# A planned order for attention ahead of a mixture of experts: two more names in the planner's port set, and attention's tables of numbers replaced

## The chip, the cores and the metric

The kernel runs on one core of a Trainium2 chip. The metric is the device time of one execution in microseconds (us). The engines are named as in the profile: PE (TensorE; PEld is its weight load), DVE (VectorE), ACT (ScalarE), POOL (GpSimd) and SP (SyncE, which here issues nearly all DMAs from one queue).

## The reference

Attention over 8 batches, 8 heads, 576 positions and 64 columns, joined with a memory, and then a layer of 8 experts with a capacity.

```
scores = scale * q @ k^T, causal;  a = exp(scores - max);  a /= a.sum + 1e-9
local = a @ v
phi(x) = where(x > 0, x, exp(x) - 1) + 1          # = max(x, 0) + exp(min(x, 0))
q_p = phi(q);  mem = (q_p @ M_prev) / (q_p . z_prev + 1e-6)
attn = g * mem + (1 - g) * local                  # g from beta, by head
x = attn as [4608, 512];  logits = x @ w_gate
experts take tokens in order of logits, 576 at most each;  out = relu(x @ w1) @ w2
```

## The kernel before, in words

Attention goes through 16 units, each half a batch (4 heads). All values are carried as two float16 parts, a high one and the low rest, so each product is made of two or three matmuls. For a unit, k, q and v are loaded (`kf`, `qf`, `vf`); k, q and phi(q) are cast to the high part, the low part is taken by a subtraction on POOL (`h<-kf,h`, `p<-ef,p`), both are turned by PE into `pb` (five PSUM banks shared by all stages) and copied to `kT`, `qT` and `pT`. The half of `qT` that holds q's high part is moved to the lower 64 partitions of `qM` (the step `qmove`), k's low part likewise to `kB` (the step `kb`). Row maxima come from PE products in `pb` and DVE reductions (`mx<-pb`, the steps MX); they are turned, cast to `mr` (the step `mfin2r`) and sent by a DMA into row 64 of `qM`. Then come the scores in `pb`, their exponentials on ACT (`ph<-pb`, `pb<-pb` or `pf<-pb`), the low parts on DVE (`pl<-pb,ph`) or POOL (`pl<-pf,ph`), the products with v (`avo`) and with the memory (`avm`), and the division and sum on DVE. The result is cast to `xs` (the step `ncast`) and written to DRAM.

Four small steps matter for what follows. `phr` writes relu(-q) into `ef`; `phe` (ACT) takes the exponential of its negative and `phs` (DVE) adds max(q, 0), which gives phi. `mh` casts the merged memory and z to float16 on 64 partitions; `mh2` copies that to the other 64; `ml` subtracts it for the low part.

The order is made by a planner in the kernel's own program. Each step is a node with its inputs, alternatives of engine with a planned duration each, and a priority. `Sched.run` places the nodes one after the other on planned clocks: among those that could start within `tol` ns of the earliest it takes the lowest priority. The order so found is the order of the instructions on every engine; at run time each engine only waits for its data. Priorities come from tables (`off` by step, `dl` by unit and step), the engine of a step with alternatives from `pin` (one letter for each use in a unit: a = ACT, v = DVE, p = POOL, d = a DMA of SP, * = the planner chooses, by durations and `bias`). Unit 0 has no pins.

The planner also holds DVE and POOL apart. For a step whose name is in the set `LK`, a start on DVE is not placed before POOL's last planned step has ended (`poolb`), and POOL's next is not placed before that step's end (`lockV`). Steps whose names are not in `LK` are planned on DVE as if POOL were not there.

The expert layer is a second plan with tables of its own, which follows attention's.

Of the kernel before, what the change touches and what calls it, by code (L numbers as in the profile page):

```python
# [24 lines left out]
          'kba': -38256.38,  # L25
          'kbd': -26666.66,
          'kbv': -40060.57,
          'kha': 14508.09,
          'khp': 79231.15,
          'khv': 24617.63,  # L30
          'klp': -1086.28,
          'klv': 16564.27,
          'mh2a': 20115.95,
          'mh2v': -71452.4,
          'mha': 22820.34,
          'mhv': 89368.52,
          'mlp': -31325.33,
          'mlv': 98087.6,
          'mra': 17856.1,
          'mrv': -40742.45,  # L40
          'mza': 48409.13,
          'mzv': 168176.88,
          'nap': -923.34,
          'nav': -3267.9,
          'nca': -18457.66,
          'ncp': 25373.91,
          'ncv': -21886.13,
          'nsp': -32165.33,
          'nsv': -132.24,
          'p2p': 3448.83,  # L50
          'p2v': -5.41,
          'p4sp': -101839.76,
          'p4sv': 7041.96,
          'pha': -31945.75,
          'php': 29271.45,
          'phra': -17422.93,
          'phrv': 21464.53,
          'phv': -15662.98,
          'plp': -19639.54,
          'plv': 43456.26,  # L60
          'prepca': -6518.9,
          'prepcv': -117462.96,
          'qha': -48927.36,
          'qhp': 53729.35,
          'qhv': -70868.4,
          'qlp': 66042.22,
          'qlv': 67290.35,
          'qmovea': 37764.26,
          'qmoved': 9935.43,
          'qmovev': -17228.33,  # L70
          'tea': -3203.28,
          'tev': -3567.68,
          'vha': -7856.47,
          'vhp': 10605.02,
          'vhv': 49945.15,
          'vlp': 20772.25,
          'vlv': 26630.93,
          'xtea': -71403.73,
          'xtev': 179859.67},
 'dl': {'0': {'AV': 146.09,  # L80
              'MX': -624.92,
              'N': -126.83,
              'P2': 205.25,
              'S': -143.66,
              'fin1': 261.98,
              'fin2': 110.94,
              'kb': -92.85,
              'kh': -1057.1,
              'kl': -799.26,
              'kt': 409.38,  # L90
              'lk': -815.63,
              'lm': -128.09,
              'lq': -615.68,
              'lv': 17.6,
              'maxrem': -253.86,
              'mfin': 482.24,
              'mfin2': 105.89,
              'mfin3': -298.67,
              'mh': -569.13,
              'ml': 141.3,  # L100
              'mz': -906.61,
              'nadd': -161.05,
              'ncast': 1096.75,
              'nsub': -761.84,
              'ph': -9.18,
              'phe': -815.32,
              'phr': 503.82,
              'phs': 98.73,
              'pl': -713.0,
              'prep': 158.29,  # L110
              'proc24': 786.98,
              'pt': 498.84,
              'qh': -300.16,
              'ql': -10.8,
              'qmove': 271.64,
              'qt': -259.45,
              'sj4': -1617.95,
              'vh': 583.59,
              'vl': 580.19},
        '1': {'AV': -25.95,  # L120
              'MX': -64.68,
              'N': -535.37,
              'P2': -147.0,
              'S': 748.22,
              'fin1': 664.4,
              'fin2': -3.45,
              'kb': 238.53,
              'kh': -839.21,
              'kl': 952.34,
              'kt': 230.67,  # L130
              'lk': -445.86,
              'lm': -581.61,
              'lq': -148.4,
              'lv': 20.94,
              'maxrem': 246.5,
              'mfin': -687.39,
              'mfin2': 22.77,
              'mfin3': -21.79,
              'mh': -646.37,
              'ml': 320.58,  # L140
              'mz': 193.71,
              'nadd': -884.82,
              'ncast': -314.9,
              'nsub': 431.22,
              'ph': 77.88,
              'phe': -364.63,
              'phr': -979.48,
              'phs': 202.3,
              'pl': 390.55,
              'prep': 112.67,  # L150
              'proc24': 17.02,
              'pt': 120.82,
              'qh': -827.23,
              'ql': 1226.18,
              'qmove': 922.01,
              'qt': -359.08,
              'sj4': -517.69,
              'vh': -449.25,
              'vl': -525.9},
        '10': {'AV': 733.61,  # L160
               'MX': -9.55,
               'N': -43.6,
               'P2': -27.07,
               'S': 120.09,
               'fin1': -121.61,
               'fin2': 528.74,
               'kb': 308.28,
               'kh': 579.55,
               'kl': 231.8,
               'kt': -310.65,  # L170
               'lk': -985.15,
               'lm': 22.19,
               'lq': -760.75,
               'lv': 653.54,
               'maxrem': 832.59,
               'mfin': -154.75,
               'mfin2': -103.77,
               'mfin3': 164.76,
               'mh': 1180.68,
               'ml': -110.56,  # L180
               'mz': 442.55,
               'nadd': -95.12,
               'ncast': 113.49,
               'nsub': -253.87,
               'ph': 370.77,
               'phe': 1372.58,
               'phr': -862.17,
               'phs': 266.25,
               'pl': -166.72,
               'prep': 671.38,  # L190
               'proc24': 43.6,
               'pt': -134.43,
               'qh': 380.29,
               'ql': 824.81,
               'qmove': 110.84,
               'qt': -905.38,
               'sj4': -117.53,
               'vh': 1303.13,
               'vl': 73.67},
        '11': {'AV': 392.77,  # L200
               'MX': -119.89,
               'N': 107.93,
               'P2': -1287.85,
               'S': 537.41,
               'fin1': 559.45,
               'fin2': 175.23,
               'kb': -23.13,
               'kh': -316.63,
               'kl': 316.7,
               'kt': -267.79,  # L210
               'lk': 1004.46,
               'lm': 317.64,
               'lq': 927.07,
               'lv': -555.69,
               'maxrem': -231.11,
               'mfin': 53.44,
               'mfin2': -28.5,
               'mfin3': -375.62,
               'mh': 289.75,
               'ml': -252.17,  # L220
               'mz': -107.18,
               'nadd': 309.19,
               'ncast': -1234.73,
               'nsub': 691.93,
               'ph': -604.12,
               'phe': -723.96,
               'phr': -499.8,
               'phs': -516.33,
               'pl': 169.21,
               'prep': -551.37,  # L230
               'proc24': 438.49,
               'pt': -289.42,
               'qh': 420.7,
               'ql': 540.55,
               'qmove': 441.27,
               'qt': -164.57,
               'sj4': 108.12,
               'vh': -419.32,
               'vl': -35.56},
        '12': {'AV': 92.79,  # L240
               'MX': 85.32,
               'N': 713.16,
               'P2': -217.09,
               'S': -90.99,
               'fin1': 335.64,
               'fin2': 663.47,
               'kb': 1548.9,
               'kh': 225.74,
               'kl': -192.86,
               'kt': -292.84,  # L250
               'lk': -226.47,
               'lm': -572.91,
               'lq': -787.24,
               'lv': 475.0,
               'maxrem': 222.28,
               'mfin': 289.39,
               'mfin2': 383.96,
               'mfin3': 442.07,
               'mh': 272.14,
               'ml': 221.9,  # L260
               'mz': 444.22,
               'nadd': -589.26,
               'ncast': 297.69,
               'nsub': 743.62,
               'ph': -132.61,
               'phe': 153.97,
               'phr': 393.16,
# [1546 lines left out]
```

## Time and profile before

| | |
|---|---|
| time, median of 3 runs | 937.16 us (933.75 to 937.4) |
| profiled execution, its own time | 931.03 us |
| its span | 929.3 us |
| DVE busy, whole span | 693.6 us (75%) |
| PE busy, whole span | 804.9 us (87%) |
| POOL busy, whole span | 589.6 us (63%) |
| ACT busy, whole span | 579.3 us (62%) |

Attention takes the first 450 us or so, the expert layer the rest. The shares mix the two, so they are read by stage.

### The profile page before, as it was taken

To read this page: it belongs to the slowest core of one execution; us is meant where nothing else is said; L and a number is where in the kernel's file an instruction comes from. 1 tells how busy PE (TensorE), PEld (TensorE's weight loads), DVE (VectorE), ACT (ScalarE), POOL (GpSimd) and SP (SyncE) were. 2 spreads that over 40 slices of the span, in tenths; PEclk is the share of its full clock that TensorE was granted. 3 is DMA by queue.
4 is the path that set the end of the run, shared out by engine and by line. 5 is a ranking of instruction groups with operands and counts; after the bars stand their busy time and mean duration, and the time that the engine had idled before them with its cause. 6 is when DMAs were issued, how large, how long until landed. Compare 5 with 4: busy or idle time off the path is not lost.

```text
span 929.3 us, 25223 instructions
## 1 busy us (share of the span) xinstructions
PE 804.9 (87%) x9736; PEld 517.6 (56%) x9736; DVE 693.6 (75%) x2319; ACT 579.3 (62%) x1053; POOL 589.6 (63%) x595
## 2 busy tenths in 40 slices
PE   4687888799898899999416999999999899999996
PEld 3475767578677677778305444454444444444442
DVE  7999998999999999988789878787767675102020
ACT  4485969688688689889326684848284655653120
POOL 7959789798889799688304382928274545762101
PEclk9899999999999999999656999999999999999999
DMA  5665665456655537433315274656462819940101
GB/s 129 138 142 130 141 143 113 82 135 135 145 135 125 123 67 154 82 84 60 79 33 200 89 201 155 185 179 174 143 186 103 238 29 245 239 169 12 40 13 40
DMA packets 230302, 116.49 MB, mean 125 GB/s; under 512 B 199013, under 2 KB 208229, under 8 KB 230181
## 3 DMA queue, kind: packets, MB, share of 16 engines
q1 hardware_dynamic: 224293, 96.00, 42.2%
q0 software_dynamic: 5888, 18.88, 6.4%
q8 instruction: 76, 1.25, 0.6%
q14 instruction: 45, 0.37, 0.1%
HBM read 72.40 MB, written 18.87 MB: 98 GB/s over the span
## 4 chain that ended last, share of the span: by engine, by line
PE 49%; DVE 20%; issue 12%; ACT 7%; POOL 5%; DMA 5%; SPq 1%; POOLq 0%; DVEq 0%; ACTq 0%
PE py L1461 15%; PE ph L1461 15%; PE pb L963 8%; DVE mx L1119 6%; PE avo L963 4%; PE pb L1105 2%; DVE scr L1697 2%; DVE pl L1261 2%; PE prem L1461 2%; DMA xT<-xs 2%; ACT ph L1256 2%; ACT pb L1260 1%; PE pr L1461 1%; PE avm L963 1%; POOL out_dram L1675 1%
## 5 line engine op out<-in xcount | busy, mean ns | idle before, releaser
L1613 POOL TENSOR_TENSOR wl<-wst,wh 128x1024 f16<-128x1024 f32 x62 | 131.4, 2141 | 83.8 <-ACT wh L1612 76.2
L1461 PE MATMUL ph<-xT,wh 128*128 128x512 f16 (+1 forms) x560 | 164.3, 366 | 2.1 <-DVE hl L1656 2.1
L1256 ACT ACTIVATE ph<-pb 128x512 f16<-128x512 f32 x192 | 116.3, 606 | 27.3 <-PE pb L963 24.0
L1119 DVE TENSOR_REDUCE mx<-pb 128x1 f32<-128x512 f32 (+3 forms) x256 | 123.0, 543 | 2.4 <-PE pb L963 2.2
L1675 POOL DMA_INDIRECT out_dram<-ys,idx x40 | 39.0, 974 | 119.8 <-ACT ys L1670 101.8
L963 PE MATMUL pb<-qT,kT 128*128 128x64 f16 (+3 forms) x576 | 102.2, 243 | 13.2 <-DVE pl L1261 4.6
L1656 DVE SCALAR_TENSOR_TENSOR hl<-ph,hh 128x512 f16<-128x512 f32 x64 | 44.1, 689 | 81.8 <-ACT hh L1655 76.7
L963 PE MATMUL avo<-V,ph 128*128 128x65 f16 x1792 | 102.3, 194 | 1.5 <-DVE xt L1322 1.3
L1461 PEld LDWEIGHTS <-wh 128*128 128x128 f16 x1072 | 68.7, 99 | 59.8 <-issue 4.3
L963 PE MATMUL avo<-V,pl 128*128 128x65 f16 x896 | 98.1, 197 | 1.4 <-POOL pl L1264 1.4
L963 PE MATMUL pb<-qM,kB 128*128 128x64 f16 (+3 forms) x576 | 97.5, 242 | 0.8 <-DMA qM<-mr 0.8
L1461 PE MATMUL ph<-xT,wl 128*128 128x512 f16 (+1 forms) x280 | 98.1, 365 | 0.0
L1461 PE MATMUL py<-wh,hh 128*128 128x512 f16 x256 | 97.0, 379 | 1.3 <-ACT hh L1655 1.1
L1461 PE MATMUL py<-wl,hh 128*128 128x512 f16 x256 | 97.0, 379 | 0.0
L963 PE MATMUL pb<-kT,qM 128*128 128x256 f16 (+5 forms) x384 | 82.4, 315 | 16.6 <-DVE mx L1119 10.1
L1461 PE MATMUL prem<-xT,wh 128*128 128x64 f16 x512 | 96.6, 193 | 0.0
L963 PEld LDWEIGHTS <-ph 128*128 128x128 f16 x1792 | 92.6, 99 | 6.5 <-issue 3.4
L1261 DVE TENSOR_TENSOR pl<-pb,ph 128x512 f16<-128x512 f32 x128 | 86.4, 678 | 9.9 <-ACT pb L1260 9.2
L1264 POOL TENSOR_TENSOR pl<-pf,ph 128x512 f16<-128x512 f32 x64 | 75.4, 1178 | 22.8 <-ACT pf L1263 22.8
L1655 ACT ACTIVATE hh<-ph 128x512 f16<-128x512 f32 x64 | 38.0, 594 | 80.7 <-PE ph L1461 59.3
L1697 DVE TENSOR_SCALAR_CACHE_REDUCE scr<-p_LwT,th 128x320 f16<-128x320 f32 x168 | 85.0, 544 | 2.7
L963 PEld LDWEIGHTS <-pl 128*128 128x128 f16 x896 | 85.2, 99 | 1.5 <-POOL pl L1264 1.5
(286 smaller groups left out, 2246.5 us busy)
## 6 DMA issues: line engine op xcount, KB each, us to landing
wst<-in_moe_w_dram SPq DMA_DIRECT2D x32, 1024.0 KB
kf<-in_k_dram SPq DMA_DIRECT2D x64, 128.0 KB
qf<-in_q_dram SPq DMA_DIRECT2D x64, 128.0 KB
vf<-in_v_dram SPq DMA_DIRECT2D x64, 128.0 KB
xd<-xs SPq DMA_DIRECT2D x16, 512.0 KB
kB<-kT SPq DMA_DIRECT2D x15, 288.0 KB
kf<-in_k_dram SPq DMA_DIRECT2D x32, 32.0 KB
qf<-in_q_dram SPq DMA_DIRECT2D x32, 32.0 KB
```

The costliest lines, as they stand in the source:

```text
L963: def MM(*a,**kw): mm(*a,skip_group_check=True,**kw)
L1105: for i in range(a,b_): nc.tensor.transpose(p[:,128*(i-a):128*(i-a)+128],g()[:,i],cst['idh'])
L1119: R=lambda o,i: nc.vector.tensor_reduce(o,i,axis=mybir.AxisListType.X,op=ALU.max)
L1256: c=SC.add('Eh',[('A',478)],lambda x,a=a: nc.scalar.activation(phs_[x.buf['ph']][:,0:512],pbb[a.buf['pb']],AF.Exp,scale=0.125),acq=('ph',) ...
L1261: e=SC.add('P2v',[('V',602)],lambda x,a=a,c=c: nc.vector.tensor_sub(pls_[c.buf['ph']][:,0:512],pbb[a.buf['pb']],phs_[c.buf['ph']][:,0:512] ...
L1264: e=SC.add('P2',[('P',1113)],lambda x,c=c,d=d: nc.gpsimd.tensor_sub(pls_[c.buf['ph']][:,0:512],pfs[d.buf['pf']],phs_[c.buf['ph']][:,0:512] ...
L1461: def MM(*a,**kw): mm(*a,skip_group_check=True,**kw)
L1613: SC.add('sp',[('P',2079)],lambda x,ws=ws,k=k,s=s: G_.tensor_sub(wl[:,k,s],ws(),wh[:,k,s]),r=[key+('h',)],w=[key+('l',)],after=[b],rel=rel ...
L1655: b=SC.add('hh',[('A',478)],lambda x,a0=a0,f=f: A_.activation(hh[:,f],phb[a0.buf['ph']],AF.Relu),w=[('hh',f)],after=[y],prio=pr('hh',n,pos ...
L1656: SC.add('hl',[('V',602)],lambda x,a0=a0,f=f: V_.scalar_tensor_tensor(hl[:,f],phb[a0.buf['ph']],0.0,hh[:,f],op0=ALU.max,op1=ALU.subtract), ...
L1675: SC.add('scat',[('P',1250 if i<4 else 1200,'p',0,(1250,'n'))],lambda x,e=e,i=i,r_=r_: G_.indirect_dma_start(out=outv[5*n+i],out_offset=ba ...
L1697: V(462,lambda x,j=j,t_=t_,c_=c_: V_.tensor_scalar(scr[j],LwT,t_[:,j+1:j+2],0.0,op0=ALU.is_ge,op1=ALU.add,accum_out=c_[:,j:j+1]),r=['LwT', ...
```

## The change

Two names are added to `LK`: `phr` and `mh2`. (`phs`, the sum itself, is not in the set before or after.) All of attention's tables are replaced: `bias`, `dl`, `off`, `pin`, and `tol`, which goes from 13.3 to 0. The expert layer's tables and all other code stay, and so does the number of instructions of every kind of work; some change engine.

```diff
-LK={'rc','qh','kh','vh','gt', ... ,'mh','sp','thu','base'}
+LK={'rc','phr','mh2','qh','kh','vh','gt', ... ,'mh','sp','thu','base'}
...
- 'pin': {'kb': 'd*ad',
+ 'pin': {'kb': 'd*va',
...
-         'mh2': 'a',
-         'ml': '*',
-         'mr': 'a',
+         'mh2': '*',
+         'ml': 'v',
+         'mr': 'v',
...
-         'nc': 'paap',
+         'nc': 'papp',
...
-         'phr': 'v',
+         'phr': 'a',
...
-         'qmove': 'a*d*',
+         'qmove': 'd*dv',
...
- 'run': {'tol': 13.3},
+ 'run': {'tol': 0},
...
- 'off': {'AV': 354.36,
+ 'off': {'AV': 932.62,
```

What this does to the engines, counted over the whole program (all in attention):

| step | rows | before | after |
|---|---|---|---|
| `phr`, 128x1152 | 15 | DVE | ACT |
| `qmove`, 64x2304 | 15 | ACT | DMA of SP |
| `mfin2r` (`mr`), 18x128 | 15 | ACT | DVE |
| `mh2`, 64x260 | 15 | ACT | DVE (16 of 16 there now) |
| `ml`, 64x260 | 15 | POOL | DVE (1 of 16 stays on POOL) |
| `ncast` (`xs`), 128x320 | 15 | 12 ACT, 3 DVE | POOL |
| copies out of `pb` to `kT`, `qT`, `pT`, 128x1024 | 5 | DVE | ACT |
| the same to `kT`, 128x256 | 8 | DVE | ACT |
| `kb` of unit 0, 64x512 | 2 | ACT | DVE |
| `p_LwT`, at the end of attention | 2 | ACT | DVE |

The order moves nearly everywhere; three places follow. On DVE before, where unit 8's `phr` stands, in the midst of attention (`avm`, `avo` and `de` are the divisions of an earlier head, `mx` the maxima of unit 8):

```order
L1261 TENSOR_TENSOR pl_144<-pb_176,ph_136 128x512
L1168 TENSOR_TENSOR mx_157<-mx_157,pb_178 128x2
L1188 TENSOR_SCALAR ef_112<-qf_108 128x1152
L1308 TENSOR_TENSOR xt_163<-avm,de_162 128x320
L1261 TENSOR_TENSOR pl_140<-pb_175,ph_132 128x512
L1006 COPY qT_122<-pb_178 128x1024
```

And on ACT after, where unit 8's `phr` stands now:

```order
L1256 ACTIVATE ph_133<-pb_178 128x512
L1188 ACTIVATE ef_112<-qf_108 128x1152
L1260 ACTIVATE pb_178<-pb_178 128x512
L1256 ACTIVATE ph_134<-pb_177 128x512
L1192 ACTIVATE pb_175<-ef_112 128x512
```

The 15 rows of `phr` have left DVE, and stand among the exponentials on ACT.

On DVE after, at the tenth of the places where `ml` and `mh2` stand, some two thirds through attention's rows:

```order
L1261 TENSOR_TENSOR pl_146<-pb_175,ph_138 128x512
L1261 TENSOR_TENSOR pl_147<-pb_178,ph_139 128x512
L1199 TENSOR_TENSOR ml_131<-mf_127,mh_129 64x260
L1199 TENSOR_TENSOR ml_130<-mf_126,mh_128 64x260
L1006 COPY mh_129<-mh_129 64x260
L1006 COPY mh_128<-mh_128 64x260
L1006 COPY kT_118<-pb_178 128x1024
```

Two units' `ml` and `mh2` stand here together. The 31 rows of `ml` and `mh2` on DVE after stand in 20 such places, alone or two to four together (rows with at most two others between them are counted as one place); before, DVE had one of them.

On ACT before, where a `qmove` stands, and on SP after, where one stands now (`qM<-qM` resets a row of the same tile, `kB<-kT` is the step `kb`, `xd<-xs` writes a result, `kf`, `qf` and `vf` are loads):

```order
L1256 ACTIVATE ph_138<-pb_179 128x512
L1260 ACTIVATE pb_179<-pb_179 128x512
L1005 COPY qM_99<-qT_122 64x2304
L1005 CAST p_117<-ef_112 128x18x64
L1005 CAST mh_129<-mf_127 64x260
L1256 ACTIVATE ph_139<-pb_176 128x512
```

```order
L1116 DMA qM_100<-qM_100 1x16x144
L1110 DMA kB_96<-kT_119 64x2304
L1114 DMA qM_100<-qT_123 64x2304
L1344 DMA xd<-xs_167 128x4x512
L1023 DMA kf_107<-in_k_dram 128x4x64 x4
```

The copy has left ACT's row of exponentials and stands in SP's queue, mostly behind the two other DMAs of the same pair of tiles.

## Rows read from the trace of the kernel before

**Rows 1.** Windows: busy us of PE, PEld, DVE, ACT, POOL; clock, DMA share, GB/s.

```profile
150.00:200.00 50.00, 41.88 (x789) 34.19 (x786) 47.72 (x128) 38.62 (x72) 41.23 (x48) 0.97 0.57 123
200.00:250.00 50.00, 45.75 (x850) 37.11 (x850) 48.13 (x126) 37.04 (x68) 45.62 (x47) 1.00 0.59 130
250.00:300.00 50.00, 45.32 (x866) 36.93 (x865) 48.32 (x132) 43.04 (x83) 45.20 (x46) 1.00 0.59 131
300.00:350.00 50.00, 44.54 (x817) 35.90 (x817) 48.20 (x119) 38.11 (x71) 42.58 (x43) 1.00 0.44 97
350.00:400.00 50.00, 46.51 (x892) 38.08 (x890) 48.64 (x133) 41.73 (x81) 41.31 (x43) 1.00 0.57 112
```

**Rows 2.** Groups of instructions, 0 to 450 us: count, busy us, mean ns, idle before.

```profile
L1188 DVE TENSOR_SCALAR ef<-qf 128x1152 f32<-128x1152 f32 x15 | 22.4, 1493 | 0.3 <-POOL p L1096 0.3
L1006 DVE COPY kT<-pb 128x1024 f16<-128x1024 f16 x27 | 18.3, 681 | 0.7 <-PE pb L1105 0.4
L1006 DVE COPY kT<-pb 128x256 f16<-128x256 f16 x15 | 4.1, 275 | 1.2 <-PE pb L1105 1.2
L1006 DVE CAST xs<-xt 128x320 f16<-128x320 f32 x3 | 1.4, 479 | 0.0
L1006 DVE COPY mh<-mh 64x260 f16<-64x260 f16 x1 | 1.1, 1109 | 0.0
L1006 DVE COPY kB<-kT 64x640 f16<-64x640 f16 x2 | 0.6, 313 | 0.0
L1006 DVE CAST mrx<-pb 8x128 f16<-8x128 f32 x2 | 0.5, 274 | 0.4 <-PE pb L1171 0.4
L1378 DVE TENSOR_TENSOR p_big<-Lw,p_m 128x256 f32<-128x256 f32 x1 | 0.4, 406 | 0.0
```

**Rows 3.** The same view, groups that leave ACT, and one that gives ACT's price.

```profile
L1005 ACT COPY qM<-qT 64x2304 f16<-64x2304 f16 x15 | 31.6, 2111 | 5.1 <-DVE qT L1006 4.8
...
L1005 ACT CAST h<-kf 128x1152 f16<-128x1152 f32 x15 | 17.3, 1150 | 2.7 <-DMA kf<-in_k_dram 2.4
```

**Rows 4.** The tile `ef`, its instructions on DVE by L1188: ns least/median/most.

```profile
L1188 DVE TENSOR_SCALAR ef<-qf x15: 737/978/5054, 30.8 to 364.1; 128x1152 f32<-128x1152 f32 x15
```

**Rows 5.** Timeline from 171 us, DVE, then ACT, then POOL: start, us.

```profile
171.85 5.05 DVE L1188 TENSOR_SCALAR ef<-qf 128x1152 f32<-128x1152 f32 x1 [0.27 <-POOL p L1096]
...
178.53 0.60 ACT L1192 ACTIVATE pb<-ef 128x512 f32<-128x512 f32 x1 [4.36 <-DVE qT L1006]
...
171.78 0.78 POOL L1324 TENSOR_TENSOR xs<-xt,xs 128x320 f16<-128x320 f32 x1
...
175.50 0.78 POOL L1324 TENSOR_TENSOR xs<-xt,xs 128x320 f16<-128x320 f32 x1
180.18 0.46 POOL L1007 TENSOR_SCALAR xs<-xt 128x320 f16<-128x320 f32 x1 [3.90 <-DVE xt L1322]
```

**Rows 6.** Timeline of DVE, further places.

```profile
43.46 4.26 DVE L1188 TENSOR_SCALAR ef<-qf 128x1152 f32<-128x1152 f32 x1
...
88.20 0.75 DVE L1188 TENSOR_SCALAR ef<-qf 128x1152 f32<-128x1152 f32 x1
...
436.42 0.68 DVE L1261 TENSOR_TENSOR pl<-pb,ph 128x512 f16<-128x512 f32 x1
437.02 0.49 DVE L1308 TENSOR_TENSOR avo<-avo,de 128x320 f32<-128x320 f32 x1
...
458.46 0.54 DVE L1697 TENSOR_SCALAR_CACHE_REDUCE scr<-p_LwT,th 128x320 f16<-128x320 f32 x1
```

**Rows 7.** The chain that ended last, two of its pieces.

```profile
208.47 6.74 DMA xT<-xs
...
262.51 3.88 DMA qM<-qM
```

More of the change, by code (lines that the diff above doesn't have):

```diff
@@ L24 @@
           'czv': 10497.75,
[L25 to L41, printed above, removed]
@@ L42 @@
-          'mzv': 168176.88,
+          'kba': -31478.93,
+          'kbd': -993.6,
+          'kbv': -67297.36,
+          'kha': -87315.47,
+          'khp': 111947.67,
+          'khv': 150540.47,
+          'klp': -64455.31,
+          'klv': 21427.71,
+          'mh2a': -10148.73,
+          'mh2v': -129058.78,
+          'mha': 10062.42,
+          'mhv': 200975.97,
+          'mlp': -20170.51,
+          'mlv': 117999.35,
+          'mra': -19706.74,
+          'mrv': -83652.35,
+          'mza': 15800.11,
@@ L43 @@
+          'mzv': 112057.9,
           'nap': -923.34,
           'nav': -3267.9,
[L45 to L49, printed above, removed]
+          'nca': -45720.67,
+          'ncp': 47954.34,
+          'ncv': 11844.42,
+          'nsp': -70781.66,
+          'nsv': 582.29,
           'p2p': 3448.83,
           'p2v': -5.41,
-          'p4sp': -101839.76,
-          'p4sv': 7041.96,
-          'pha': -31945.75,
@@ L55 @@
[L55 to L72, printed above, removed]
@@ new lines @@
+          'p4sp': 40625.76,
+          'p4sv': 48405.6,
+          'pha': -48271.2,
+          'php': 38853.08,
+          'phra': -58268.18,
+          'phrv': 34654.36,
+          'phv': 32370.4,
+          'plp': -56694.44,
+          'plv': -12027.31,
+          'prepca': 26516.98,
+          'prepcv': -32356.81,
+          'qha': -28630.82,
+          'qhp': 116967.98,
+          'qhv': -116320.55,
+          'qlp': 75817.56,
+          'qlv': 78410.89,
+          'qmovea': 24209.02,
+          'qmoved': 30919.98,
@@ L723 @@
  'npf': 4,
- 'off': {'AV': 354.36,
-         'MX': -71.76,
-         'N': 35.4,
-         'P2': -404.5,
-         'S': 79.95,
-         'fin1': 1411.67,
-         'fin2': 45.35,
-         'kb': -155.13,
-         'kh': -864.76,
-         'kl': -325.66,
-         'kt': -45.19,
-         'lk': 36.12,
-         'lm': 5.45,
-         'lq': 24.59,
-         'lv': -52.41,
-         'maxrem': 69.93,
-         'mfin': 533.74,
-         'mfin2': -740.97,
-         'mfin3': -1009.04,
-         'mh': 367.78,
-         'ml': -815.85,
-         'mz': 581.35,
-         'nadd': 89.93,
-         'ncast': 229.29,
-         'nsub': 716.8,
-         'ph': -250.69,
-         'phe': 1029.76,
-         'phr': 1761.5,
-         'phs': 219.4,
-         'pl': 1360.18,
-         'prep': -1283.21,
-         'proc24': 1390.48,
-         'pt': 95.92,
-         'qh': -614.21,
-         'ql': -1858.34,
-         'qmove': -829.71,
-         'qt': -301.43,
-         'sj4': -153.0,
-         'vh': -344.36,
-         'vl': -365.2},
@@ L764 @@
- 'p2k': 'vpvpvvvvpvpv',
- 'pin': {'kb': 'd*ad',
-         'kh': 'a',
-         'kl': '*pp',
-         'mh': '*',
-         'mh2': 'a',
-         'ml': '*',
-         'mr': 'a',
+ 'off': {'AV': 932.62,
+         'MX': -251.07,
+         'N': -207.16,
+         'P2': -819.74,
+         'S': 168.87,
+         'fin1': 1549.22,
+         'fin2': -121.63,
+         'kb': 341.34,
+         'kh': -1117.01,
+         'kl': -744.18,
+         'kt': -79.69,
+         'lk': 108.87,
+         'lm': 240.67,
+         'lq': 55.75,
+         'lv': 426.09,
+         'maxrem': 262.96,
+         'mfin': 864.51,
+         'mfin2': -1214.22,
+         'mfin3': -3518.74,
+         'mh': 411.95,
+         'ml': -530.46,
+         'mz': 705.32,
+         'nadd': -782.1,
+         'ncast': 635.81,
+         'nsub': 1506.01,
+         'ph': -1619.83,
+         'phe': 1349.27,
+         'phr': 2893.53,
+         'phs': 72.17,
+         'pl': 2050.6,
+         'prep': -149.5,
+         'proc24': 1323.23,
+         'pt': -172.99,
+         'qh': -791.93,
+         'ql': -1614.46,
+         'qmove': -2408.6,
+         'qt': -330.43,
+         'sj4': -212.64,
+         'vh': -1990.62,
+         'vl': -92.65},
@@ L772 @@
+ 'p2k': 'vpvpvvvvpvpv',
+ 'pin': {'kb': 'd*va',
+         'kh': '*',
+         'kl': 'pp*',
+         'mh': 'a',
+         'mh2': '*',
+         'ml': 'v',
+         'mr': 'v',
          'mz': 'a',
          'na': 'vp*v',
-         'nc': 'paap',
-         'ns': '***p',
+         'nc': 'papp',
+         'ns': '**pp',
          'p2': 'ppvpvv**pvpp',
-         'p4s': '*',
-         'ph': 'a',
+         'p4s': 'p',
+         'ph': '*',
          'phh': 'a',
          'phl': 'pp',
-         'phr': 'v',
@@ L782 @@
-         'pl': '***',
-         'prepc': 'a',
+         'phr': 'a',
+         'pl': 'p*v',
+         'prepc': 'v',
          'qh': 'p',
-         'ql': 'ppv',
-         'qmove': 'a*d*',
-         'te': '**v*vva**avv',
+         'ql': 'ppp',
+         'qmove': 'd*dv',
+         'te': '****vva**aaa',
          'vh': 'p',
          'vl': 'p*p',
-         'xte': '***v'},
- 'run': {'tol': 13.3},
+         'xte': '*aav'},
+ 'run': {'tol': 0},
  'strict': 1,
@@ L814 @@
     __slots__=('i','nm','alts','fn','deps','prio','dma','acq','rel','nleft','succ','rdy','start','fin','buf','var','eng','done','slack','wg','lag','xl','strict')
-LK={'rc','qh','kh','vh','gt','lg4','prep','P2','kl','ql','pl','vl','nadd','nsub','kb','qmove','p4s','ml','mh','sp','thu','base'}
+LK={'rc','phr','mh2','qh','kh','vh','gt','lg4','prep','P2','kl','ql','pl','vl','nadd','nsub','kb','qmove','p4s','ml','mh','sp','thu','base'}
 class Sched:
```

1297 lines of the change are left out of this document (650 added, 647 removed).

## The prediction

> **What bounds the kernel now.** The expert layer's plan and tables stay, so a gain or loss has to be made in attention, whose end is taken here as the first count of the expert layer's search on DVE, at 458.5 us [rows 6]. The view by stretch is read first [rows 1]: from 150 to 400 us DVE is busy for 241.0 of 250 us and idle for 9.0, while PE is busy for 224.0, POOL for 215.9 and ACT for 198.5. In that part DVE sets the pace.
>
> DVE's busy time isn't all work, and the second view shows it. The step `phr` takes 22.4 us in 15 rows, 1.49 us each [rows 2], but its least is 0.737 and its median 0.978 us, its most 5.05 [rows 4]. The same tile shape can't cost seven times as much by itself. At the worst place, 171.85 us, the row on DVE lasts as long as POOL's unbroken run, five instructions from 171.78 to 176.28, and ends when POOL has a pause [rows 5]; the row at 43.46 is its like with 4.26 us [rows 6]. So this step, which reads and writes SBUF alone, waits for POOL on DVE, and the wait is recorded as its duration. What follows from it is in the same rows: after it ACT has stood for 4.36 us and POOL for 3.90. Of the 22.4 us, 15 x 0.737 = 11.1 are work and 11.3 are such waits, 7.8 of them in two rows (4.26 + 5.05 - 2 x 0.74).
>
> **The change, part by part.** Rows on DVE overlap by 0.08 us: 0.68 us is followed after 0.60 [rows 6]. So each row costs its mean less 0.08.
>
> Taken off DVE [rows 2]: `phr`, 15 x 1.41 = 21.2 us; five 128x1024 copies out of `pb`, 5 x 0.60 = 3.0; eight 128x256 ones, 8 x 0.195 = 1.6; three casts to `xs`, 3 x 0.40 = 1.2. Together 27.0 us.
>
> Put on DVE, without waits for POOL [rows 2]: `mr`, 15 casts of an 18x128 tile out of PSUM, nearest the cast to `mrx` at 0.274: 15 x 0.19 = 2.9. `ml`, 15 subtractions of 260 columns, nearest the 256-column `p_big` at 0.406, also with both inputs in SBUF: 15 x 0.33 = 5.0. `mh2`, 15 float16 copies of 260 columns. The only row of it takes 1.109 us, far more than the 0.313 of 640 columns in the `kB` copy, so it holds a wait; between nothing and 0.23 a row, I take 0.13: 2.0 (0 to 3.5). Two `kb` copies at 0.22 and two copies to `p_LwT`, 0.9 together. That is 10.8, so DVE is left with 16.2 us less before waits.
>
> The waits are the unknown. `ml` and `mh2` read and write SBUF alone, as `phr` does, and I count both as waiting alike; `mr` reads PSUM, as the 0.68 us rows do, which show no such spread. Their 31 rows stand in 20 places, and behind the first of a place the others mostly follow in the same pause. What a place costs is bounded by `phr`'s rows [rows 4]: the median wait is 0.978 - 0.737 = 0.24 us, the mean 0.76. At 0.24 the places cost 4.8 us, at 0.76 they cost 15.1. The rows were planned into pauses of POOL, which `phr` wasn't; but POOL is busy for 86% of 150 to 400 us, and on the chip the pauses aren't where the plan has them. I take 0.40, nearer the median, since the mean is made by two rows of fifteen: 8.0 us. DVE's sum is then 16.2 - 8.0 = 8.2 us less (1.1 to 11.4).
>
> By the Trainium skill (SBUF — State Buffer, Who interferes with whom) the pair of ports that DVE and GpSimd share is a lock held for one instruction, and whoever issues first goes first; a tensor_tensor with both inputs in SBUF contends too. By that a place would wait for the rest of one POOL instruction at most, an estimate of 0.4 us from POOL's rows here, and the sum would hardly differ. The trace agrees that a DVE row blocks, and goes further: it waited through five POOL instructions in a row, not one [rows 5]. The sum goes by the rows.
>
> ACT loses 31.6 us of `qmove` and gains 15 `phr` at the 1.15 us of a cast of that shape, 17.3 us [rows 3]; what else changes there (15 `mr`, 15 `mh2` and 12 casts out, 13 copies in) is short and stands on both sides. It comes out some 14 us lighter or more. It is idle for a fifth of 150 to 400 us, so this lies off the path; what it brings is that a 2.11 us copy no longer stands in front of exponentials. I cost it at nothing, and if exponentials did wait behind `phr`, each would wait 1 us less long than behind `qmove`. POOL loses 15 `ml` and gains 15 `xs`, small against its 86%, taken as nothing too.
>
> `qmove` on SP costs an issue there and a landing. The nearest rows are the small DMA `qM<-qM`, 3.88 us on the chain from issue to use [rows 7], against 2.11 on ACT. It is hidden where DVE has other rows between the last copy to `qT` and the unit's first maximum. In the new order these are 11 to 23 rows at the places that I counted, or 5 us and more. I cost it at nothing; without the cover it is a rival, below.
>
> The new order itself can't be priced row by row. It starts unit 0 alike and ends alike, with the same last steps. Of DVE's 8.2 us, I let 0.8 become time, since 9 us of its pauses remain and PE is at 45 of 50 in the same stretches: 6.6 us. On the profiled execution's own 931.0 us that makes 924.4 (span 922.7). The median of the runs shown lies 6.1 above that execution, and from the median the forecast is 937.2 - 6.6 = 930.6.
>
> **The rivals.** (1) The time stays. DVE's saving goes into waits for others: PE is busy for 91% between 200 and 400 us, and the chain of waits changes hands at almost each step. For it speaks that ACT and PE have little room at the end of attention; against it that PE still has 17.9 us idle in those 200. Time 935 to 940.
>
> (2) Slower, by DVE waiting for POOL. Each of the 30 rows of `ml` and `mh2` that came to DVE waits for itself, as long as `phr` did on the mean: 30 x 0.76 = 22.8 us, 16.2 - 22.8 = 6.6 more than now, 944. It decides from 16.2 / 20 = 0.81 us a place. Two or three rows like that at 171.85 would do it. For it speaks that POOL runs unbroken for 4 us and more; against it that 6 of 15 `phr` rows lasted 0.75 us or less, like that at 88.20 [rows 6], without a wait, though planned as if POOL weren't there.
>
> (3) Slower, by SP. Each `qmove` now stands behind a `qM<-qM` and a `kB` DMA, sometimes behind a transpose, whose stay on the chain is up to 6.74 us [rows 7]. If in every unit the first maximum waited for the difference of 3.88 and 2.11, that would be 15 x 1.8 = 27 us; if in four units, 7 us, which eats the gain. It decides from about four units. The 11 rows of cover speak against it.
>
> (4) The words on the change are not all in it. `phr` in `LK` can't act in units 1 to 15, where it is pinned to ACT, and `phs`, the sum, isn't in the set. Whatever is gained comes from the moved steps and the order; this alters no price above.
>
> (5) The new order is better or worse elsewhere, in ways that the counts don't show. Better by 10 us or more: 927 or less. Worse: 942 and above.
>
> **How the numbers follow.** What a measurement of this kernel can tell from no change is about 0.5%, 4.7 us. The forecast holds with 0.45, rival 1 with 0.23, rival 2 with 0.12, rival 3 with 0.06; rival 5 better 0.08, worse 0.06. The likeliest alone lies between 937.2 - 11.4 = 925.8 and 937.2 - 1.1 = 936.1. The range over all reaches from 921, half way into the better orders, to 943, just below rival 2's full price. Faster by over 0.5% (under 932.5): 0.45 + 0.08 = 0.53. Within: 0.23. Slower: 0.12 + 0.06 + 0.06 = 0.24. The forecast's upper part, above 932.5, and the lower part of rival 1 balance roughly.
>
> **What would show it.** Right: no row of `phr` on DVE; the sum of DVE's busy time up to attention's end smaller by some 8 us; the first row of the expert layer's search (L1697) some 6 or 7 us earlier; rows of `ml` on DVE at a mean under 0.8 us, of `mh2` under 0.6. Wrong by rival 2: such rows of 3 to 5 us, with ACT and POOL idle behind them. Wrong by rival 3: PE or DVE waiting for the DMA `qM<-qT`, or `qM<-qT` in the chain. Wrong by rival 1: DVE's busy time falls and its idle time grows as much. If the expert layer's part, from the first L1697 to the end, changes by more than 2 us, part of the difference isn't attention's.

## The result, and the profile after

| | before | after |
|---|---|---|
| time, median (12 runs each) | 934.96 us (928.8 to 941.84) | 942.0 us (933.82 to 947.83) |
| ratio after to before, 95% interval | | 1.0067 (1.0044 to 1.0091) |
| profiled span | 929.3 us | 941.5 us |

The change made the kernel slower by 0.67%, some 6 us; the forecast was 930.6 us. The time after lies inside the range given, but the time rose where it was forecast to fall. The profiled execution of before was some 4 us under its median, so the two traces show a larger difference (12.2 us) than the ratio does. Where a price matters below, it comes from ratios, and the end of attention in the traces stands beside it.

The first thing read is where the time went. The search of the expert layer starts on DVE at 467.27 us, where before it started at 458.46 [rows 6]: 8.8 of the 12.2 us are attention's.

Timeline of DVE after, the end of attention (start, us, engine, line, operation):

```profile
467.27 0.54 DVE L1697 TENSOR_SCALAR_CACHE_REDUCE scr<-p_LwT,th 128x320 f16<-128x320 f32 x1
```

Windows from the start to this row, of before and then of after (busy us of PE, PEld, DVE, ACT, POOL with their counts, granted clock, DMA share, GB/s):

```profile
0.00:458.46 458.46, 386.83 (x6927) 311.23 (x6927) 422.39 (x1115) 341.95 (x643) 380.33 (x453) 0.97 0.54 119
```

```profile
0.00:467.27 467.27, 390.36 (x6927) 313.47 (x6927) 417.39 (x1133) 317.96 (x609) 373.74 (x453) 0.96 0.59 126
```

DVE has 5.0 us less to do in attention, ACT 24.0 and POOL 6.6, and attention still takes longer. DVE's idle time rose from 36.1 to 49.9 us. So the loss isn't work; it is a wait.

The groups of the moved steps (count, busy us, mean ns, idle before), 0 to 460 us:

```profile
L1188 ACT ACTIVATE ef<-qf 128x1152 f32<-128x1152 f32 x15 | 17.5, 1169 | 7.6 <-POOL p L1096 4.4 <-DMA qf<-in_q_dram 3.1
L1199 DVE TENSOR_TENSOR ml<-mf,mh 64x260 f16<-64x260 f32 x15 | 9.9, 670 | 0.0
L1006 DVE COPY mh<-mh 64x260 f16<-64x260 f16 x16 | 4.8, 312 | 0.4
L1006 DVE CAST mr<-pb 18x128 f16<-18x128 f32 x15 | 4.0, 271 | 3.2 <-PE pb L1171 3.2
```

These came out near their forecast prices, waits for POOL included (the last number of a group is the engine's idle time before it). The view of waits (0 to 460 us: us in total, times, longest) shows what is new:

```profile
ACT ph L1256 <- PE pb L963: 46.6, 13, 7.1
...
DVE mx L1119 <- PE pb L963: 12.9, 11, 2.7
...
PE pb L963 <- DMA qM<-qT: 8.5, 7, 2.0
...
PEld L963 <- DMA qM<-qT: 3.9, 4, 1.9
```

Read from the bottom up, PE stands for 8.5 us at seven places until the DMA `qM<-qT`, the step `qmove`, has landed. PE's weight load waits at four of the same places, so its 3.9 us don't add to that (9.2 us where both are counted once, not 12.4). DVE's maxima then wait for PE. ACT's exponentials wait for PE too, and for longer, but that row isn't `qmove`'s: it hardly falls when `qmove` is left out (second group of experiments). In before the two waits for PE were 24.0 and 2.2 us, and none was for `qM<-qT` (waits, 0 to 460 us, of before; the row in the middle is needed below):

```profile
ACT ph L1256 <- PE pb L963: 24.0, 16, 4.7
...
DVE pl L1261 <- ACT pb L1260: 9.2, 17, 1.6
...
DVE mx L1119 <- PE pb L963: 2.2, 4, 0.9
```

The chain that ended last holds the DMA in six places, 26.5 us together, in the form in which [rows 7] had `qM<-qM`:

```profile
by line: DVE mx L1119 13.5%; PE pb L963 10.5%; DMA xT<-xs 7.7%; DMA qM<-qT 5.8%; PE avo L963 5.3%; issue 5.2%; DVE pl L1261 4.0%; PE pb L1105 3.5%; POOL pl L1264 2.8%; POOL xs L1324 2.3%; POOL p L1096 2.1%; POOL V L1208 2.0%; SPq L1023 1.9%
...
59.70 4.12 DMA qM<-qT
...
322.51 4.51 DMA qM<-qT
...
376.32 4.89 DMA qM<-qT
```

One place in the timeline of after, DVE, SP's queue and PE (a row marked SPq is the time that SP needs to issue a DMA; [1.57 <-DMA qM<-qT] is idle time and what ended it):

```profile
319.53 0.88 DVE L1006 COPY qT<-pb 128x1024 f16<-128x1024 f16 x2
...
319.54 1.55 SPq L1023 DMA_DIRECT2D qf<-in_q_dram  x2
321.14 0.62 SPq L1081 DMA_DIRECT2D mf<-in_M_prev_dram  x1
321.87 0.54 SPq L1023 DMA_DIRECT2D qf<-in_q_dram  x1
322.51 0.51 SPq L1114 DMA_DIRECT2D qM<-qT  x1
...
327.07 0.39 PE L963 MATMUL pb<-kT,qM 128*128 128x512 f16 x1 [1.57 <-DMA qM<-qT]
327.56 1.16 DVE L1119 TENSOR_REDUCE mx<-pb 128x1 f32<-128x512 f32 x2 [1.68 <-PE pb L963]
```

The last copy to `qT` ends at 320.41. SP is then in the midst of issuing loads back to back, and comes to `qmove` at 322.51, 2.10 us later. The data are in use 4.56 us after that. Between the copy and the first maximum DVE has 18 other rows, as the plan had it, and they are used up 1.68 us too early.

Over the 15 moves the issue on SP comes 0.03 to 3.46 us after the last copy to `qT` (17.8 us together), and the first product of the maxima mostly 4.2 to 5.5 us after the issue.

### The profile page after: what moved, and what is told of

Same layout as the page of the kernel before. It is cut to its first block, busy times and chain, and to the rows that moved or that the text cites. A ratio compares the mean times of both kernels' runs of the same rounds, so it can differ in the third digit from the quotient of the medians.

```text
span 941.5 us, 25283 instructions
## 1 busy us (share of the span) xinstructions
PE 810.6 (86%) x9736; PEld 521.6 (55%) x9736; DVE 688.6 (73%) x2337; ACT 555.6 (59%) x1020; POOL 583.2 (62%) x595
## 4 chain that ended last, share of the span: by engine, by line
PE 43%; DVE 21%; issue 11%; DMA 9%; POOL 9%; ACT 3%; SPq 2%; another core or an unknown queue 0%; POOLq 0%; DVEq 0%; ACTq 0%
PE py L1461 15%; PE ph L1461 14%; DVE mx L1119 7%; PE pb L963 5%; DMA xT<-xs 4%; DMA qM<-qT 3%; PE avo L963 3%; DVE scr L1697 2%; PE prem L1461 2%; DVE pl L1261 2%; PE pb L1105 2%; POOL pl L1264 1%; POOL xs L1324 1%; POOL p L1096 1%; POOL V L1208 1%
## 5 line engine op out<-in xcount | busy, mean ns | idle before, releaser
L1256 ACT ACTIVATE ph<-pb 128x512 f16<-128x512 f32 x192 | 116.9, 610 | 53.5 <-PE pb L963 46.6
L1119 DVE TENSOR_REDUCE mx<-pb 128x1 f32<-128x512 f32 (+3 forms) x256 | 123.0, 544 | 13.0 <-PE pb L963 12.9
L963 PE MATMUL pb<-kT,qM 128*64 128x64 f16 (+5 forms) x384 | 83.6, 319 | 26.9 <-DVE mx L1119 10.3
```

The lines of the kernel that those rows point to most:

```text
L963: def MM(*a,**kw): mm(*a,skip_group_check=True,**kw)
L1119: R=lambda o,i: nc.vector.tensor_reduce(o,i,axis=mybir.AxisListType.X,op=ALU.max)
L1256: c=SC.add('Eh',[('A',478)],lambda x,a=a: nc.scalar.activation(phs_[x.buf['ph']][:,0:512],pbb[a.buf['pb']],AF.Exp,scale=0.125),acq=('ph',) ...
```

## The experiments

All are compared with the kernel before on the same chip. Time is the median; the ratio has its 95% interval. In the label, a_ and same_ stand for the changed kernel, b_ for the one before. The kernels that leave a step out work on an old tile and don't give the reference's result; they are there for the price of the step. Where a step is sent to another engine, the plan and the order stay, and only the engine that the step is emitted on changes:

```diff
-    for x in order: x.fn(x)
+    for x in order:
+        if x.nm in AT and x.var in AT[x.nm]: x.var=AT[x.nm][x.var]
+        x.fn(x)
```

| kernel | from | edit | us | ratio |
|---|---|---|---|---|
| a_qmove_act | after | `AT={'qmove':{'d':'a'}}` | 939.08 | 1.0130 (1.0100 to 1.0160) |
| b_qmove_dma | before | `AT={'qmove':{'a':'d'}}` | 954.49 | 1.0287 (1.0253 to 1.0321) |
| b_phr_act | before | `AT={'phr':{'v':'a'}}` | 926.8 | 1.0008 (0.9989 to 1.0028) |
| b_moved_to_dve | before | the same, and `mfin2r`, `mh2`, `ml` to DVE | 940.18 | 1.0153 (1.0120 to 1.0185) |
| after_again | after | none | 943.04 | 1.0073 (1.0045 to 1.0101) |
| a_no_qmove | after | no `qmove` in units 3 to 15 | 933.49 | 0.9951 (0.9927 to 0.9976) |
| b_no_qmove | before | no `qmove` in units 3 to 15 | 935.1 | 0.9978 (0.9953 to 1.0003) |
| b_no_phr | before | no `phr` in units 2 to 15 | 927.48 | 0.9910 (0.9887 to 0.9933) |
| a_late_land | after | planned again, `qmove` ready 1.5 us later | 939.2 | 1.0130 (1.0108 to 1.0152) |
| a_plan_act | after | planned again, `qmove` pinned to ACT | 937.22 | 1.0105 (1.0084 to 1.0126) |
| a_qmove_actq | after | `qmove` DMA issued by ACT | 925.54 | 0.9984 (0.9964 to 1.0005) |
| a_old_engines | after | before's engines for the five steps | 957.62 | 1.0326 (1.0301 to 1.0351) |
| a_moves_actq | after | `qmove`, `qM<-qM`, `kB<-kT` issued by ACT | 931.74 | 1.0088 (1.0058 to 1.0119) |
| a_kbmz_actq | after | `qM<-qM`, `kB<-kT` issued by ACT | 926.4 | 1.0013 (0.9992 to 1.0034) |
| b_qmove_actq | before | `qmove` as a DMA issued by ACT | 939.51 | 1.0181 (1.0154 to 1.0207) |
| same_after | after | none | 943.53 | 1.0083 (1.0051 to 1.0114) |
| same_actq | after | as a_qmove_actq | 938.11 | 0.9999 (0.9971 to 1.0026) |
| same_no_qmove | after | as a_no_qmove | 932.95 | 0.9956 (0.9926 to 0.9985) |

The rows fall into five groups, each on one chip with its own runs of before: the first four (before at 925.84 us), the next four (937.92), four (926.17), three (925.13) and the last three (936.46).

**First: one step at a time between the two kernels.**

a_qmove_act: 

> The changed kernel in its own order, with the 15 copies of the step qmove put back on ACT (2.11 us each) at the place where their DMA was issued; nothing else moves. Theory SP (the late DMA of qmove makes the maxima late): the chain loses its pieces of 4.1 to 4.9 us on that DMA, and the time falls by 6 us or more against the changed kernel, to about the kernel before. Theory ORDER (the new order is worse whatever carries qmove): no change within 2 us, or slower by some of the 31.6 us that ACT gets back.

b_qmove_dma: 

> The kernel before in its own order, with the 15 qmove copies as DMAs of SP, issued at the place of the copy. Theory SP: slower than before by 6 us or more (15 landings of about 4 us in place of 2.1, some behind loads and transposes). Theory ORDER: same as before within 3 us, or faster, since ACT loses 31.6 us.

b_phr_act: 

> The kernel before in its own order, with the 15 phr rows moved from DVE to ACT at their place. Theory of the prediction (DVE's waits for POOL cost time): DVE is rid of 22.4 us with 11.3 us of waits, and the time falls by 5 to 15 us. Rival (DVE's saving is not time): within 3 us of before.

b_moved_to_dve: 

> The kernel before in its own order, with four of the changed kernel's moves: phr to ACT, mr, mh2 and ml to DVE. The prediction's sum gives 21.2 us off DVE and 9.9 on it before waits: faster by 3 to 9 us if the waits of ml and mh2 stay near 0.4 us; slower than the run with phr alone by the 10 us and the waits. If ml and mh2 wait as phr did on the mean in this order, that was not planned for them, no gain is left.

With `qmove` on SP, the old order loses 2.9%. PE and its weight load wait longer than in any other run, 32.6 us where both are counted once:

```profile
PE pb L963 <- DMA qM<-qT: 29.8, 11, 6.0
...
PEld L963 <- DMA qM<-qT: 20.0, 7, 6.1
```

But the copies aren't welcome on ACT either where the new order has its DMAs: 1.013. There the low parts on DVE wait for ACT's second exponential, 18.0 us against 9.2 in before (waits, 0 to 460 us, of a_qmove_act):

```profile
DVE pl L1261 <- ACT pb L1260: 18.0, 18, 2.3
```

Taking `phr` off DVE and giving it to ACT, the step that the forecast rested on, gained nothing in the old order. And `mr`, `mh2` and `ml` on DVE at places not planned for it cost 1.5% less 0.1%, some 13 us. `ml` takes 762 ns there on the mean, 670 in the new order.

**Second: leave one step out.** after_again repeats the changed kernel as the measure for its neighbours.

after_again: 

> The changed kernel as it is, on one chip with the three that follow, so that they can be compared. All theories: 0.4 to 0.9% slower than before.

a_no_qmove: 

> The changed kernel, with the copies of qmove of units 3 to 15 (13 DMAs) left out: these units take their maxima and scores from an old tile. No engine gets anything in their place. Theory SP: the late landings go, and the time falls by 8 us or more against the changed kernel, below the kernel before. Theory ORDER: by 3 us at most; the changed kernel stays slower than before less its own qmove.

b_no_qmove: 

> The kernel before, with the copies of qmove of units 3 to 15 (13 rows of ACT, 27 us) left out in the same way. If ACT has the room that its busy share suggests: 3 us less or nothing. If ACT's 2.11 us rows stand in the path of the exponentials: 8 us or more less. Its distance to the same run of the changed kernel is what the two orders differ by without qmove: Theory SP says about 0 to 3 us, or in favour of the changed one; Theory ORDER says 6 us or more against it.

b_no_phr: 

> The kernel before, with phr of units 2 to 15 (14 rows of DVE, some 20 us with their waits) left out; phi is then made of an old tile. The prediction's theory (DVE paces attention, its time is the kernel's time at 0.8): 12 us or more less. Rival (a full DVE doesn't set the pace, the chain of waits does): 5 us less or nothing; then the run with phr on ACT, which gave no change, had no gain to lose to ACT.

This is the account of the change. In the new order `qmove` costs 1.0073 - 0.9951 = 1.22%, 11.4 us; in the old one, as 13 copies on ACT, 0.22%, 2.1 us, with an interval that reaches nothing. The exchange costs 9.4 us. Without `qmove` in either, the new kernel is 0.27% or 2.5 us faster than the old, which is within the noise of the two. That 9.4 - 2.5 gives the loss measured on this chip (0.73%, 6.8 us) proves nothing, since the ratios add up so by themselves. The traces, one execution each, speak independently of them: attention ends at 468.92 us in after_again and 455.61 in a_no_qmove, at 458.46 in before and 457.15 in b_no_qmove, so `qmove` takes 13.3 us in the new order and 1.3 in the old. These prices hold all that goes with the move: its issue, its landing, and what its place in SP's queue does to other transfers.

The waits tell which rows were its doing (waits, 0 to 460 us, of a_no_qmove):

```profile
ACT ph L1256 <- PE pb L963: 43.7, 13, 7.1
...
DVE mx L1119 <- PE pb L963: 1.6, 2, 1.0
```

The wait of the maxima goes, from 12.9 us to 1.6; the wait of ACT's exponentials stays at 43.7 of 46.6. That one belongs to the new order, in which ACT has 24.0 us less to do.

The 14 rows of `phr` on DVE were worth 0.9% or 8.4 us by the ratio, 4.2 us by the end of attention (454.30 us in b_no_phr).

**Third: queue or landing, and the planner.**

a_late_land: 

> The changed kernel, planned again with one number changed: the planner is told that what the qmove DMA carries is ready 1.5 us later than it assumed (units 1 to 15). Engines and tables stay. Theory L (the loss of the change is the unhidden landing of qmove, 9.4 us more than the copy on ACT costs): the planner puts other work between the DMA and the first maximum, PE's idle time ended by the DMA qM<-qT falls from 12.4 us to 6 or less, and the time falls by 4 to 9 us against the changed kernel, to a ratio of 0.998 to 1.003 with the kernel before. Rival (the tables were found for the assumed landing, and any other plan with them is worse): the waits fall, but the time stays at a ratio of 1.007 or goes above it.

a_plan_act: 

> The changed kernel, planned again with qmove pinned to ACT (15 copies of 2.1 us that the planner knows of and can plan around), phr on ACT too. Theory L: the DMA's 11.4 us go and a planned copy's 2 us come, so the time is 7 to 9 us under the changed kernel, a ratio of 0.997 to 1.000. Rival (ACT has no room at these places for 27 us more, as the unplanned copies showed with 1.013): 1.007 or more, with ACT's rows ending the waits of PE and DVE.

a_qmove_actq: 

> The changed kernel, same order, the 15 qmove DMAs issued from ACT's queue in place of SP's. It parts the wait for SP's queue from the landing. If the wait behind other DMAs in SP's queue (0 to 3.5 us, median 1.2, after the last copy to qT) is the main part, the time falls by 4 us or more against the changed kernel, to 1.003 or less. If the landing (over 4 us from issue to the first product) is the main part, the time stays within 2 us, 1.005 to 1.009. If the issue costs ACT much, it is above 1.009.

a_old_engines: 

> The changed kernel's order of steps, with the engines of before for qmove (ACT), phr (DVE), mr and mh2 (ACT) and ml (POOL), each at the place that the new order gives it. It tells whether the new order is good with any engines or only with its own. If the order by itself is better (the changed kernel without qmove was 2.5 us under before), 0.997 to 1.000. If order and engines belong together, 1.013 or more, as with the qmove copies alone.

a_qmove_actq changes one word in one line:

```diff
-nc.sync.dma_start(out=qM[u%3][0:64,a:b_],in_=qTs[U3][64:128,a:b_])
+nc.scalar.dma_start(out=qM[u%3][0:64,a:b_],in_=qTs[U3][64:128,a:b_])
```

The same place in its timeline, DVE, SP's queue, ACT's queue and PE:

```profile
317.20 0.88 DVE L1006 COPY qT<-pb 128x1024 f16<-128x1024 f16 x2
...
317.46 1.58 SPq L1023 DMA_DIRECT2D qf<-in_q_dram  x2
318.12 0.47 ACTq L1114 DMA_DIRECT2D qM<-qT  x1
319.09 0.97 SPq L1081 DMA_DIRECT2D mf<-in_M_prev_dram  x1
...
323.25 0.38 PE L963 MATMUL pb<-kT,qM 128*128 128x512 f16 x1
```

The copy to `qT` ends at 318.08 and the DMA is issued 0.04 us later, while SP goes on issuing its loads. The landing is hardly shorter (3.6, 4.6 and 4.6 us for the three moves whose landing shows), but PE doesn't wait for it any more; over the 15 moves the issue comes 2.9 us late together, where it was 17.8. No wait for `qM<-qT` is left in the waits; PE has 2.4 us at two places for `qM<-qM`.

SP's queue also has 15 issues less, and that helps others. The DMA `qM<-mr`, which brings the maxima that the scores need, was issued 22.9 us late together after the casts to `mr` in the changed kernel (19.9 in after_again, 9.3 in before), and 17.8 us late here. So the gain needn't all be `qmove`'s own.

Planning again didn't help. With a later landing in the plan (a_late_land) the time for which PE or its weight load stands for `qM<-qT` fell from 9.2 to 3.2 us, as theory L had it, and the time rose to 1.013, as its rival had it. a_plan_act, which has no such DMA at all, came to 1.0105. That the tables fit one plan alone is argued from these two runs, not shown. And a_old_engines, the new order with the old engines, is the slowest of all. So the new order isn't better by itself.

**Fourth: how far this holds.**

a_moves_actq: 

> The changed kernel, same order, with all three small moves between SBUF tiles issued from ACT's queue: qmove, the reset qM<-qM (13) and the kb part that is a DMA (kB<-kT, 15). With qmove alone there the kernel stood at 0.9984, and the chain of waits showed the reset (4.65 and 5.73 us) and kB<-kT (3.83 and 4.45 us) in its place. If their wait in SP's queue costs as qmove's did, 2 to 5 us come off: 0.993 to 0.997. If those waits are their landing, the time stays at 0.997 to 1.000. If 43 issues of 0.47 us on ACT begin to count, 1.001 or more.

a_kbmz_actq: 

> The changed kernel, same order, qmove still in SP's queue, the reset qM<-qM and kB<-kT issued from ACT's. It parts qmove's own wait from the load of SP's queue. These two stood right ahead of qmove at some of the places (0.6 us each), so if it is the load ahead that counts, some of qmove's wait goes: 1.001 to 1.004. If it is the wait for whatever else stands ahead (loads, results, transposes), 1.005 to 1.008 as the changed kernel.

b_qmove_actq: 

> The order of before with the 15 qmove copies taken off ACT and issued as DMAs from ACT's queue, at the places of the copies. From SP's queue the same gave 1.0287. If the wait in SP's queue is the cost, most of it goes: 1.002 to 1.010, the landing of 4.6 us against a copy of 2.1 being what is left. If the landing is the cost, 1.020 or more.

With two other small moves taken out of SP's queue and `qmove` left there (a_kbmz_actq), its issue is 8.0 us late together in place of 17.8, and the ratio is 1.0013. So most of the gain comes without touching `qmove`, although PE or its weight load still stands for it for 8.6 us in place of 9.2. What this run shows is that the load of SP's queue costs time, and not only by `qmove`: `qM<-mr` is 14.2 us late together here, as against 22.9. Which transfers the gain goes to wasn't parted.

All three on ACT's queue are worse (1.0088), a miss: the issue is prompt (3.7 us late together), yet PE or its weight load stands for the landing for 8.3 us. Waits, 0 to 460 us, of a_moves_actq:

```profile
PE pb L963 <- DMA qM<-qT: 7.7, 6, 2.1
...
PEld L963 <- DMA qM<-qT: 5.6, 3, 2.3
```

Its `qmove` and `kB<-kT`, 288 KB each, now share ACT's queue, and the one landing of each that shows took 5.0 us. That they hold each other up there isn't shown: in a_kbmz_actq, where they stand in two queues, the two landings of `qmove` that show took 5.8 and 6.0 us, and that kernel is faster. Why this run loses stays open.

In the old order ACT's queue took 1.0287 to 1.0181, somewhat over a third of the cost. PE or its weight load still stands for 9.6 us, where it was 32.6. The result lies between the two bounds expected. By the ratios what SP's queue doesn't explain is the larger part there; by the end of attention (496.15 us from SP's queue, 476.39 from ACT's, 458.46 in before) it is about half.

**Last: the three steps of the ladder on one chip,** since the chips differ by 1% in the kernel before.

same_after: 

> The changed kernel as it is, beside the next two on one chip, since the chips differ by about 1% in the time of the kernel before (926 and 937 us) and the changed kernel was timed on the slower ones alone, the version with ACT's queue on a faster one. If ratios carry over from chip to chip: 1.005 to 1.010.

same_actq: 

> The changed kernel with the 15 qmove DMAs issued from ACT's queue, on the same chip. If the wait in SP's queue costs what the two chips showed: 0.996 to 1.001, and 0.006 to 0.011 under the changed kernel here. If that difference was one of chips, within 0.003 of it.

same_no_qmove: 

> The changed kernel with the qmove of units 3 to 15 left out (their maxima and scores come from an old tile), on the same chip: 0.993 to 0.998. What is left between it and the version with ACT's queue is what the move costs without SP's queue: 0.001 to 0.005 if the landing of 4.6 us is nearly hidden, above 0.005 if it isn't.

Between the changed kernel and the one with ACT's queue lie 0.84% or 7.9 us by the ratios, 5.4 by the medians (whose intervals leave some 4 us either way); between that and no `qmove` 0.43%, 4.0 us, or 5.2 by the medians. In the traces, one execution each, attention ends at 468.88, 464.65 and 455.46 us, which makes 4.2 and 9.2; the execution traced of same_actq was the slowest of its twelve, and a_qmove_actq, on the faster chip, had 461.67. The time for which PE or its weight load stands for `qM<-qT` goes from 9.6 us to this (waits, 0 to 460 us, of same_actq):

```profile
PE pb L963 <- DMA qM<-qT: 0.2, 1, 0.2
```

So issuing `qmove` from SP's queue costs 4 to 8 us of the 11 to 13 that `qmove` costs in the new order. By the whole time that is as large as the loss, since with ACT's queue the kernel is level with the one before. Whether the queue or what is left is the larger part, these runs can't tell.

## Why the prediction was wrong

**The step that failed is "`qmove` on SP ... I cost it at nothing".** Measured, it costs 11.4 to 11.9 us by the ratios, against 2.1 us for the copies on ACT. The working had two errors. It took the landing from a DMA of 4.5 KB (3.88 us [rows 7]), where this one moves 288 KB and takes 4.1 to 4.9 us on the chain. And it counted cover from the last copy to `qT`, as if the DMA were issued then, where SP comes to it 0.03 to 3.46 us later. The 11 to 23 rows of DVE were there, "5 us and more"; needed were a wait in the queue, 1.2 us in the median, and about 4.5 us of landing, 6.7 us together at the place shown. What one more DMA does to the others in SP's queue wasn't weighed at all.

Rival 3 had named the queue, the landing and the marks that would show them (PE waiting for `qM<-qT`, the DMA in the chain). Its middle price, four units for 7 us, is of the size of the 9.4 us that the exchange cost; seven units waited. It got 0.06, because the count of rows was held against it without adding up issue and landing.

**The saving on DVE came within its bounds; what it is worth was overrated.** DVE's sum up to attention's end fell by 5.0 us, forecast 8.2 with bounds of 1.1 and 11.4. The waits of `ml` and `mh2`, over their least times of 354 and 217 ns, are 9.9 - 15 x 0.354 = 4.6 and 4.8 - 16 x 0.217 = 1.3 us, 5.9 in all where 8.0 was taken; rival 2 didn't come. But the sentence "in that part DVE sets the pace", and the factor of 0.8 built on it, were too strong. b_no_phr frees DVE of 17.9 us and gains 8.4 by the ratio, 4.2 by the end of attention: a factor of 0.5 at most. All that the change does beside `qmove` is worth 2.1 to 2.5 us, not clear of noise, where 6.6 were forecast.

Leaving `phr` out is worth 8.4 us and moving it to ACT nothing, although it frees DVE alike: attention's DVE sum is 404.52 us in b_no_phr and 404.19 in b_phr_act, down from 422.39. By the end of attention the two are 8.0 us apart as well (454.30 and 462.28). What differs is 15 rows of 1.17 us on ACT, "off the path" in the forecast, and with them DVE waits longer for ACT's second exponential (waits, 0 to 460 us, of b_no_phr and then of b_phr_act):

```profile
DVE pl L1261 <- ACT pb L1260: 10.3, 19, 1.6
```

```profile
DVE pl L1261 <- ACT pb L1260: 15.4, 23, 1.6
```

So ACT's idle share isn't free room here. Not all of the 8 us need be ACT's time, since leaving `phr` out also spares `phe` the wait for it; no run parts the two.

**Rivals 4 and 5.** No run has the new names in `LK` with the old tables, so what they do to the order stays open. Rival 5 is settled in part: order and engines belong together (a_old_engines), and the order isn't better apart from them.

**The expert layer's part** went from 470.8 to 474.2 us, beyond the 2 us that the prediction allowed. The plan there is the same, and without `qmove` the changed kernel showed 480.3 and 473.4 us on two occasions, so this is spread, not the change.

## What to carry to other kernels

When a copy becomes a DMA, add up two terms and not one, what stands in the issuing queue when the data are ready and the landing of a transfer of that size, and only then compare with the cover. Then ask which other transfers stand behind it. A queue that also issues the loads is busy just when the loads are, and its rows in the timeline say how late it is. A wait that shows in two rows, PE's and its weight load's, is one wait; and before a wait is put down to a cause, see whether it goes when the cause is left out. An engine busy for nine tenths isn't the pace by itself; to price a step, leave it out once, and move it once, since the two can differ by all of the gain.

The version with the 15 DMAs issued by ACT mends the change (0.9984 and 0.9999) but doesn't beat the kernel before by an amount that can be measured.

## What the runs showed of the hardware

Issuing a DMA held SP's queue for 0.37 to 2.3 us each in attention of the changed kernel (a load 0.5 us in the median), a transpose 3.1 to 5.5 us, and rows of loads, results and transposes stand there back to back. The 15 `qmove` issues on ACT took 0.47 to 0.52 us each, against 0.48 to 1.66 on SP.

The Trainium skill (DMA: Bandwidth & Descriptors, Issuing engines are not separate DMA queues) says that issuing from several engines saves only the sequencer's time to initiate a DMA, which is usually small beside the DMA itself. For one DMA by itself this case agrees: 0.5 us of issue, and a landing that stayed at 3.6 to 4.6 us. What stands in line before it isn't small here: up to 3.46 us a move, and with the relief of the other transfers 4 to 8 us of the kernel's time.

An `ml` of 0.354 us at the least took 2.28 us at 439.19 us on DVE, while POOL worked without a break, much as `phr` did before [rows 4, 5], and another 2.00 at 99.23; the other 13 took 0.60 or less.

The chips differ where the kernel doesn't: the same program (a_qmove_actq and same_actq) took 461.9 and 475.1 us for the expert layer's part (span less the start of its search, 923.6 - 461.7 and 939.7 - 464.6) at granted clocks of 0.951 and 0.948 over the execution. On the chips of the first, third and fourth group this part took 460.5 to 464.4 us in all eleven traces, on that of the second and fifth 470.8 to 480.3 in all seven. Why wasn't followed.
